# Three groups per half instead of four in the small transforms of a spectral filter, with buffers shared and the order of all engines searched anew

## The chip, the cores and the metric

One core of a Trainium2 chip runs the kernel. The metric is the device time of one execution in microseconds (us), the median of several. A core has five engines that run at the same time, each through its own list of instructions: PE (matrix multiply; its weight loads are listed apart as PEld), ACT and DVE (element by element, both can read PE's result memory PSUM), POOL, and SP, which here only issues DMA transfers. An engine takes its instructions strictly in the order of its list; where one needs the result of another engine or of a transfer, it waits for a semaphore, and everything behind it on the same engine waits too. PSUM has eight banks of 512 columns.

## What is computed

```python
x = A_x                                   # 1 x 2048 x 640, bf16
xn = (x - mean) / sqrt(var + 1e-5)        # over the 640
A = irfft2(rfft2(xn) * (w_r + 1j * w_i))  # over 2048 x 640, w_* are 2048 x 321
B = gelu(xn @ w1 + b1) @ w2 + b2          # w1 640 x 1536, w2 1536 x 640
out = x + A + B
```

## The kernel before

The 2048 rows are 16 chunks of 128 rows. `XN` is a chunk normalized, `xnT` its transpose (640 x 128, in five blocks).

Branch B: layer 1 (lines 735 to 754) goes through seven blocks of 1, 1, 2, 2, 2, 4 and 4 chunks; for each block and each of 12 units of 128 hidden columns it does five matmuls into one PSUM bank (`hps`, banks 4 to 7), and ACT writes gelu to `gT`. Layer 2 (`second`, line 905) makes a chunk's 640 outputs from the 12 hidden units, each a matmul of 512 and one of 128 columns, in four quarters of three units. A chunk in `KEEP` is summed ahead of time: its result is taken out of PSUM by DVE and added to the x that waits in float32 (line 921). For the others the last matmul of branch A is added in PSUM.

Branch A is the two-dimensional transform in steps. A-matmuls (line 724) transform the chunks along the rows, part one; `XV` holds their results. Then six B groups (line 773, `etab`) transform along the 640 columns; their results go to `Xb`. Then the small transforms: for each P of four, two C groups (line 794, `mtab`) turn `Xb` into a spectrum `Y`, DVE multiplies it by the filter (lines 819 and 823: two products into `T`, their difference and sum into `Z`), and two D groups (line 828, `ntab`) turn `Z` into `U`. A C or D group uses the 128 x 128 array as 16 tiles of 32 x 32: it is 32 matmuls in two sets of 16, of 322 columns (C) or 320 (D), one set added onto the other in four PSUM banks. ACT and DVE copy the four banks out, two instructions for C (644 columns each), four for D (512 and 128 columns). SP then transposes each half of a `U` by DMA into `XV` (line 844). When all 16 are in, six E groups (line 861, `getab`) transform back along the columns, DVE unfolds the result (lines 869, 874), and the H matmuls (line 928, `htab`) do the last step along the rows, chunk by chunk, into the PSUM banks where layer 2 may already lie; DVE adds x (line 930), and SP writes the chunk out.

Banks: B, C, D and E groups each take all four lower banks (0 to 3), so that each of them can start only when the copies of the one before it are done. Layer 1 has the upper four, layer 2 two of them at a time.

Order: nothing is scheduled while the kernel runs. Each `K.op` call makes one numbered operation; `ORDER` (line 159) lists the numbers for each engine, found by a search outside, and `Sched` (line 216) only gives out buffers and works out the semaphores. `CHAIN` (line 455) is the order of the groups on the lower banks:

```python
CHAIN = "b1 b0 c01 c00 b2 c10 d01 c11 d00 b4 b3 d10 d11 c20 c21 b5 c30 d20 d21 c31 d30 d31".split()
```

(as executed, c21 comes before c20). Between the groups PE does quarters of layer 2 and pieces of layer 1. At the start PE runs `WARM` = 38 and 12 matmuls on zeros (line 571), then a transpose of the bias b1 (line 647), then transposes chunks 0 and 1 itself (line 702, `tp`), while DVE makes the statistics of the chunks (line 661) as they land; chunks 6 to 15 are transposed by DMA (line 690, `TD`). The x for the final addition is written over `xnT` and `X` in float32 (line 897) and added to by a DMA from POOL (line 915), whose place in the order `WAVE` binds to the transposes of `U`.

Of the kernel before, what the change touches and what calls it, by code (L numbers as in the profile page):

```python
# [87 lines left out]
HOLD = 0.3  # L88
# [10 lines left out]
def mm_us(n):  # L99
    return max(n / 2400.0 + 0.0027, 0.0265)  # L100
# [24 lines left out]
class Pool:  # L125
# [34 lines left out]
    "sp": """8 12 13 14 15 16 17 18 19 25 20 43 28 46 32 31 24 23 27 33 37 164 166 29 48 179 190 177 192 38 49 42  # L160
30 44 40 39 203 205 219 217 36 34 35 47 26 45 41 524 523 548 522 547 545 521 546 569 572 571 50 51 570 595 596 594
593 622 613 658 649 639 675 685 694 757 731 711 766 748 721 782 798 791 805""",
    "pe": """115 7 52 114 112 120 118 231 234 235 270 232 237 238 273 274 271 267 268 279 280 282 283 285 286 276 243 277 240 244 241 246
# [8 lines left out]
709 763 776 746 777 764 719 778 792 785 779 786 787 780 788 793 789 794 795 796 799 800 801 802 803""",  # L172
    "act": """11 9 10 116 121 53 236 233 275 272 239 269 281 284 287 278 245 242 248 251 260 293 263 296 135 254 130 299 131 132 326 323
# [3 lines left out]
758 568 578 577 588 592 749 482 476 473 464 467 470 783 774 479 599 625 660 661 696 697 733 734 768 769""",  # L177
    "dve": """0 55 54 58 56 59 60 111 117 113 119 122 123 127 63 62 65 66 64 67 124 125 126 133 136 140 139 138 143 141 142 144
# [5 lines left out]
657 663 665 664 638 698 648 699 693 701 700 674 684 735 736 737 738 770 756 730 710 765 720 771 772 773 747 781 790 797 804""",  # L184
    "pool": """3 1 2 57 5 61 68 21 75 6 4 22 82 89 96 103 110 605 723 631 641 677 667 703 713 740 750 615 651 687 784 775
759""",
# [266 lines left out]
PRIO = {"hps": 23.0, "gelu": 27.0, "pb": 67.5, "pc": 50.5, "filt": 84.0, "ipc": 36.0, "eps": 80.0, "fin": 28.5}  # L453
AHEAD = 3
CHAIN = "b1 b0 c01 c00 b2 c10 d01 c11 d00 b4 b3 d10 d11 c20 c21 b5 c30 d20 d21 c31 d30 d31".split()
XASPLIT = ["01 23 4", "01234", "01234", "01234", "01234", "01234", "0123 4", "01 23 4"]
KEEP = (0, 2, 3, 5, 6, 8, 9, 10, 11)
HOME = tuple(sorted((KEEP + tuple(c for c in range(16) if c not in KEEP))[-8:], key=lambda c: (c not in KEEP, c)))
FOLD = (1.3, 1.8, -3.2, 66.3, 45.3, 69.8, 50.8, 17.3)
GP = (-81.0, 42.0, 4.0, 72.0, -32.0, 6.0, -9.0)  # L460
G1 = 1
WAVE = (0, 3, 0, 0, 2, 0, 0, 4, 0, 2, 0, 2, 4, 2, 2, 3)
WARM = (38, 12)


def bass_parallel_sum__spectral_gfnet__dense_activation_gelu__prompt_kernel(
# [21 lines left out]
    with ExitStack() as es:  # L488
# [48 lines left out]
        p_xn, p_x1, p_xf, p_xb, p_y, p_t, p_z, p_u = Pool(2), Pool(1), Pool(2), Pool(2), Pool(2), Pool(2), Pool(2), Pool(3)  # L537
# [37 lines left out]
        idle(WARM[0], WARM[0] * 0.103)  # L575
# [79 lines left out]
        for c0, n in [(0, 1), (1, 1)] + [(c, 2) for c in range(2, 16, 2)]:  # L655
            pr = 100 - c0 / 2
            B_mv, B_r = Buf("mv"), Buf("r")
            for c in range(c0, c0 + n):
                B_st = Buf("st")
# [8 lines left out]
        for pair in range(8):  # L668
# [10 lines left out]
            for n in range(2):  # L679
# [16 lines left out]
                for j0, j1, engs in ((0, 3, ["dve"]), (3, 5, ["act"])) if c < 2 else ((0, 5, ["dve", "act"]),):  # L696
# [8 lines left out]
                    if j0 and not c:  # L705
                        idle(WARM[1], WARM[1] * mm_us(128), gate=[tp])
# [30 lines left out]
        for bi, (c0, nt) in enumerate(BLOCKS):  # L737
            for fc in range(NFC):
                hps = Buf(f"hps{bi}_{fc}", psum, 1, ZONE["hps"])
                bg = Buf(f"gT{bi}_{fc}")  # L740
# [25 lines left out]
        def five_segs(n):  # L766
            return [("128", 4 * n * mm_us(Q4)), ("32", n * 0.12 - 0.05)]

        pb_ops, filt_ops, d_ops, v_ops = [], [], [], []
        B_v = [Buf(f"v{q}") for q in range(16)]  # L770
        B_xb = {}
        xb_at = {}
        for gi, (c0, n) in enumerate(GROUPS):
            xb = Buf(f"xb{gi}", p_xb)
# [4 lines left out]
            for i in range(n):  # L779
                B_xb[c0 + i] = xb  # L780
                xb_at[c0 + i] = lambda xb=xb, i=i: (xb.slot * 3 + i) * 2 * KP
            for v in range(2):
                K.op([("dve", dve_us(320 * n) + 0.05), ("act", act_us(320 * n) + 0.08 * n)], PRIO["pb"] - c0 / 10,
                     copy(lambda v=v, xb=xb, n=n: view(xb3, xb.slot * 6 * KP + v * (KP + 1), [[2 * KP, n], [1, 2], [2, Q4]]),
                          lambda v=v, bps=bps, n=n: psb(bps.slot + 2 * v, [[Q4, n], [512, 2], [1, Q4]])), reads=[bps], writes=[xb])
        zone = {f"b{gi}": o for gi, o in enumerate(pb_ops)}
        for P in range(4):
            two = (2 * P, 2 * P + 1)
            Ys, TBs, Zs, Us = [[Buf(f"{n}{pair}", p) for pair in two] for n, p in (("Y", p_y), ("T", p_t), ("Z", p_z), ("U", p_u))]
            tiles = [(pp, qq, hi, lo) for pp in range(2) for qq in range(2) for hi in range(2) for lo in range(2)]  # L790
            in_xb = list({id(B_xb[c]): B_xb[c] for c in range(4 * P, 4 * P + 4)}.values())
            for r in range(2):
                cps = Buf(f"cps{P}_{r}", psum, 4, ZONE["cps"])
                zone[f"c{P}{r}"] = pe([("small", 0.285)], PRIO["pc"] - P / 2 + 0.02 * r, lambda P=P, r=r, cps=cps: [
                    (psb(cps.slot + 2 * pp + hi, [[1, KP]], 0, 64 * qq + 32 * (lo ^ pp), 32),
                     part(mtab, 64 * hi + 32 * lo, 32, (P == pp == qq == hi == lo == 0) * 128 + v * 64 + r * 32, [[1, 32]]),
                     part(xb3, 64 * hi + 32 * lo, 32, xb_at[4 * P + 2 * pp + qq]() + v * KP, [[1, KP]]), v == 0, v == 1)
                    for v in range(2) for pp, qq, hi, lo in tiles],
                    reads=in_xb + [B_xbpad, B_m], writes=[cps])
                for pp, Y in enumerate(Ys):  # L800
                    K.op([("act", act_us(644)), ("dve", dve_us(644))], PRIO["pc"] - two[pp] / 5,
                         copy(lambda Y=Y, r=r: view(Yb, Y.slot * 4 * KP + r * KP, [[2 * KP, 2], [1, KP]]),
                              lambda cps=cps, pp=pp: psb(cps.slot + 2 * pp, [[512, 2], [1, KP]])), reads=[cps], writes=[Y])
# [169 lines left out]
```

## Time and profile before

| what | value |
|---|---|
| median of 3 runs | 149.65 us (149.59 to 150.43) |
| the profiled execution | 149.76 us |
| its span, first to last instruction | 147.8 us, 2.0 us lie around it |
| granted PE clock by the profile | 1.00 of full speed throughout |
| busy: PE, DVE, ACT, POOL | 142.2, 108.5, 86.5, 22.6 us |
| C groups: matmuls, mean of one | 256 of 32 x 322 columns, 301 ns |
| D groups: matmuls, mean of one | 256 of 32 x 320 columns, 308 ns |
| first layer-1 matmul, last matmul | 7.61 us, 145.1 us |

A line of the timeline has the start of a run of like instructions, its length to the end of the last, the engine, the line of the kernel, the operation, what is written from what, the shape and the number of instructions; in brackets the time the engine was idle before it, and what ended it. Neighbouring matmuls overlap in their pipeline, so the time that one holds PE is read from the start of the next. A few per cent of the matmul records can be missing. `ps<-Xb,mtab` is a C group, `ps<-Z,ntab` a D group, `ps<-etab,XV` B, `ps<-getab,XV` E, `ps<-xnT,W` layer 1, `ps<-W,gT` layer 2, `ps<-gtab,T` A, `ps<-Wf,htab` H.

### The profile page before, as it was taken

How to read it: one execution, taken by the hardware profiler on the slowest of the kernel's cores; microseconds unless marked ns; L12 is line 12 of the kernel's file. 1: busy time of each engine (PE TensorE's matmuls, PEld its weight loads, DVE VectorE, ACT ScalarE, POOL GpSimd, SP SyncE). 2: the span in 40 equal slices, each digit the busy share in tenths (PEclk: the TensorE clock that was granted, in tenths of full speed). 3: DMA queues.
4: the chain of work that ended last, by engine and by line, in shares of the span. 5: the costliest groups of instructions: out<-in, count | busy, mean ns of one | idle time of the engine just before them, and what ended most of it. 6: DMA issues, size and time to landing. Idle time of an engine off the chain costs nothing.

```text
span 147.8 us, 4200 instructions
## 1 busy us (share of the span) xinstructions
PE 142.2 (96%) x1760; PEld 93.9 (64%) x1778; DVE 108.5 (73%) x230; ACT 86.5 (59%) x161; POOL 22.6 (15%) x37
## 2 busy tenths in 40 slices
PE   7999999999999999999999999999999999999993
PEld 7889999899455455456545645555446666656572
DVE  2698999999944279699837695796202599989692
ACT  3179999789779977758366767304558244403000
POOL 1302430302200025100600004000019500000000
DMA  4999999898997631904656675995447993023315
GB/s 118 342 382 380 256 318 110 214 127 177 267 180 180 183 80 36 231 22 87 130 137 50 136 91 121 131 243 65 89 89 152 256 226 124 11 82 133 138 47 177
DMA packets 30890, 23.35 MB, mean 158 GB/s; under 512 B 19224, under 2 KB 27544, under 8 KB 30744
## 3 DMA queue, kind: packets, MB, share of 16 engines
q1 hardware_dynamic: 28336, 17.48, 50.9%
q0 software_dynamic: 2368, 5.57, 16.6%
q8 instruction: 14, 0.23, 0.6%
q10 hardware_dynamic: 168, 0.04, 0.1%
q14 instruction: 4, 0.03, 0.1%
HBM read 13.58 MB, written 2.62 MB: 110 GB/s over the span
## 4 chain that ended last, share of the span: by engine, by line
PE 94%; ACT 2%; issue 2%; DVE 0%
PE ps L546 93%; ACT gT L752 1%; PE ps L702 1%; ACT Y L557 0%; ACT xnT L557 0%; DVE W L930 0%; DVE warm L562 0%
## 5 line engine op out<-in xcount | busy, mean ns | idle before, releaser
L546 PE MATMUL ps<-xnT,W 128*128 128x256 bf16 (+2 forms) x420 | 57.8, 288 | 0.1
L546 PE MATMUL ps<-W,gT 128*128 128x128 bf16 (+3 forms) x380 | 55.2, 292 | 1.7 <-issue 1.0
L546 PEld LDWEIGHTS ps<-W,gT 128*128 128x128 bf16 x396 | 30.0, 98 | 23.9 <-issue 2.7
L546 PEld LDWEIGHTS ps<-xnT,W 128*128 128x128 bf16 x420 | 34.5, 98 | 14.9 <-issue 0.9
L752 ACT ACTIVATE gT<-ps,b1col 128x256 bf16<-128x256 f32 (+2 forms) x84 | 38.3, 508 | 9.5 <-PE ps L546 9.0
L557 ACT ACTIVATE Wf<-ps 128x960 bf16<-128x960 f32 (+1 forms) x10 | 8.5, 888 | 13.5 <-PE ps L546 13.5
L661 DVE BATCH_NORM_STATS2 stats<-X 128x6 f32<-128x320 bf16 x32 | 13.8, 473 | 2.1 <-DMA X<-in_A_x_dram 2.1
L915 POOL DMA_DIRECT2D X<-in_A_x_dram x8 | 7.1, 1134 | 44.5 <-DMA XV<-gtab 15.9
L819 DVE TENSOR_TENSOR T<-Y,Wf 128x1288 bf16<-128x1288 bf16 x16 | 12.5, 822 | 0.5 <-ACT Y L557 0.4
L558 DVE CAST Xb<-ps 128x960 bf16<-128x960 f32 (+1 forms) x7 | 7.9, 1141 | 3.9 <-PE ps L546 3.9
L915 POOL DMA_DIRECT2D xnT<-in_A_x_dram x8 | 7.5, 1742 | 19.9 <-ACT gT L752 19.9
L557 ACT ACTIVATE Y<-ps 128x644 bf16<-128x644 f32 x11 | 7.6, 705 | 5.0 <-PE ps L546 5.0
L665 POOL TENSOR_TENSOR rstd<-mv,mhalf 128x2 f32<-128x2 f32 (+1 forms) x9 | 6.3, 704 | 25.4 <-DVE mv L663 25.4
L558 DVE CAST Wf<-ps 128x640 bf16<-128x640 f32 (+1 forms) x2 | 2.0, 991 | 10.8 <-PE ps L546 10.8
L557 ACT ACTIVATE XV<-ps 128x1280 bf16<-128x1280 f32 (+3 forms) x10 | 9.3, 946 | 0.8 <-PE ps L546 0.8
L718 DVE TENSOR_TENSOR T<-T 128x128 bf16<-128x128 bf16 (+1 forms) x32 | 8.4, 308 | 0.1
L930 DVE TENSOR_TENSOR W<-ps,xnT 128x640 bf16<-128x640 f32 (+2 forms) x10 | 6.8, 688 | 2.0 <-PE ps L546 2.0
L546 PE MATMUL ps<-getab,XV 32*128 32x160 bf16 (+1 forms) x128 | 7.5, 242 | 0.0
L557 ACT ACTIVATE U<-ps 128x512 bf16<-128x512 f32 (+1 forms) x8 | 3.1, 434 | 7.5 <-PE ps L546 7.5
L921 DVE TENSOR_TENSOR X<-ps,X 128x640 f32<-128x640 f32 x8 | 6.5, 817 | 1.2 <-PE ps L546 1.2
L558 DVE CAST Y<-ps 128x644 bf16<-128x644 f32 x5 | 4.1, 828 | 4.2 <-PE ps L546 4.2
L714 DVE TENSOR_TENSOR T<-T 128x640 bf16<-128x640 bf16 x16 | 7.2, 479 | 0.1
(50 smaller groups left out, 140.7 us busy)
## 6 DMA issues: line engine op xcount, KB each, us to landing
X<-in_A_x_dram POOLq DMA_DIRECT2D x8, 320.0 KB, 4.3
xnT<-in_A_x_dram POOLq DMA_DIRECT2D x8, 320.0 KB, 7.1
W<-in_B_w_dram SPq DMA_DIRECT2D x5, 480.0 KB, 4.7
out_dram<-W SPq DMA_DIRECT2D x15, 160.0 KB, 1.8
X<-in_A_x_dram SPq DMA_DIRECT2D x7, 320.0 KB, 11.1
Wf<-in_A_w_i_dram SPq DMA_DIRECT2D x6, 160.5 KB, 4.9
Wf<-in_A_w_r_dram SPq DMA_DIRECT2D x6, 160.5 KB, 3.5
W<-in_B_w_dram SPq DMA_DIRECT2D x1, 800.0 KB, 7.9
```

The source lines that it names most:

```text
L546: ins = e.matmul(o_, lhsT=lw, rhs=rh, start=st, stop=sp_, skip_group_check=True)
L557: return e.activation(dst(), src(), ACT.Copy, scale=scale)
L558: return e.tensor_copy(dst(), src())
L661: st_op[c] = K.op([("dve", 0.393)], pr, lambda e, _, c=c, h=h: e.bn_stats(stats[:, c, 6 * h:6 * h + 6], view(X, c * D + H2 * h, [[1, H2]]) ...
L665: K.op([("pool", 0.65)], 500, lambda e, _, a=a, b=b: e.tensor_tensor(out=rstd[:, a:b], in0=mv[:, a:b, 1], in1=mhalf[:, a:b], op=ALU.pow), ...
L714: K.op([("dve", dve_us(640, 2))], pr, lambda e, _, k=k, op=op, xnv=xnv, x1v=x1v: e.tensor_tensor(out=x1v(H2 * k, [[D, 2], [1, H2]]), in0=x ...
L718: ring_ops.append(K.op([("dve", dve_us(4 * w, 2))], pr, lambda e, _, op=op, x1v=x1v, xfv=xfv, o_=o_, o0=o0, o1=o1, w=w: e.tensor_tensor(ou ...
L752: K.op([("act", act_us(128 * nt, 1))], pr + PRIO["gelu"] + GP[bi], lambda e, _, c0=c0, nt=nt, fc=fc, hps=hps: e.activation(gT[:, fc, 128 * ...
L819: filt_ops.append(K.op([("dve", dve_us(4 * KP, 2))], pr, lambda e, _, k=k, Y=Y, TB=TB, pair=pair: e.tensor_tensor(out=view(TT, TB.slot * 8 ...
L915: xo_ops[c] = K.op([("pool", 0.9)], 51 - c / 20, lambda e, _, c=c, xov=xov: e.dma_start(xov(0, D), xv[:, c, :], accum_op=ALU.add), reads=[ ...
L921: kept_ops.append(K.op([("dve", dve_us(D))], 30, lambda e, _, kps=kps, xov=xov: e.tensor_tensor(out=xov(0, D), in0=psb(kps.slot, [[1, D]]) ...
L930: K.op([("dve", dve_us(w))], 95, lambda e, _, os_=os_, fps=fps, o0=o0, w=w, xov=xov, base=base: e.tensor_tensor(out=view(W1, OST + os_.slo ...
```

## The change

- Each half (two P, four pairs) has three C and three D groups instead of four of each: a first of 484 columns (all 322 of the first spectrum part of one P and 162 of its second part), a middle one of 320 (the remaining 160 columns of both P), a last one of 484. Every group is 64 matmuls in four sets of 16, and four PSUM banks as before. Names are c00, c01, c02 for the first half and c10, c11, c12 for the second; the middle one is done first in the first half.
- The copies out become 968 columns for the wide groups; 640 for the middle one of C, which writes two `Y` at once. In D a wide copy is two instructions (768 and 192 columns), a middle one four (256, 64, 256, 64).
- `Z` is written over `Y`; `Y` has four buffers, `Zb` is gone. `xnT` serves as a third `Xb` buffer (after layer 1 of chunks 0 to 3; two memsets on POOL, after the same, clear its padding) and as a fourth `U` buffer (after layer 1 of chunks 4 and 5).
- `KEEP` has ten chunks instead of nine: 0 leaves, 12 and 13 come in. The float32 x of chunks 12 and 13 lies in `xnT` where the C groups of the second half read last, that of chunk 0 where a `U` was.
- The second warm-up has 6 matmuls instead of 12. The copies of A's results are split for other pairs (`XASPLIT`).
- `ORDER`, `CHAIN`, `WAVE` and the priorities are from a new search. On the lower banks PE now does b2 b1 b0 c01 c00 c02 b5 b3 d02 d01 d00 b4 c10 c11 c12 d10 d11 d12, then E. The last four y-copies that DVE makes are those of e0 to e3 (two before). PE transposes chunks 0 and 1 ahead of the bias. SP issues b2bc ahead of x6, one mirror and one direct load of the filter ahead of x8, and x10, w2_0 and ntab ahead of x14. POOL adds x for chunks 0, 14, 12, 13, 7, 15 last.

```diff
-CHAIN = "b1 b0 c01 c00 b2 c10 d01 c11 d00 b4 b3 d10 d11 c20 c21 b5 c30 d20 d21 c31 d30 d31".split()
+CHAIN = "b2 b1 b0 c01 c00 c02 b5 b3 d02 d01 d00 b4 c10 c11 c12 d10 d11 d12".split()
-KEEP = (0, 2, 3, 5, 6, 8, 9, 10, 11)
+KEEP = (2, 3, 5, 6, 8, 9, 10, 11, 12, 13)
-WAVE = (0, 3, 0, 0, 2, 0, 0, 4, 0, 2, 0, 2, 4, 2, 2, 3)
-WARM = (38, 12)
+WAVE = (4, 0, 0, 0, 2, 0, 0, 4, 1, 0, 0, 1, 4, 1, 1, 4)
+WARM = (38, 6)
...
-        Yb = sb("Y", [128, 2 * 4 * KP])
+        Yb = sb("Y", [128, 4 * 4 * KP])
-        Zb = sb("Z", [128, 2 * 4 * KP])
...
+        def xbt(slot):
+            return (xnT, 0) if slot == 2 else (xb3, slot * 6 * KP)
+        K.op([("pool", 0.1)], 60, lambda e, _: e.memset(view(xnT, KP - 2, [[2 * KP, 3], [1, 3]]), 0.0), writes=[B_xbpad], after=l1_tiles(0, 4))
...
+        CUT = 162
+        for h in range(2):
+            Ps, pairs = (2 * h, 2 * h + 1), [4 * h + i for i in range(4)]
...
+            def c_unit(cps, P, r, k0, n, at, v, first, last):
+                return [(psb(cps.slot + 2 * pp + hi, [[1, n]], at, 64 * qq + 32 * (lo ^ pp), 32),
...
+                t, o_ = ((gtab, 0), (TT, 16 * KP), (U2, 0), (xnT, 4 * D))[U.slot]
...
+            for g in range(3):
+                cps = Buf(f"cps{h}_{g}", psum, 4, ZONE["cps"])
+                units = [(Ps[0], 1, CUT, KP - CUT, 0), (Ps[1], 1, CUT, KP - CUT, KP - CUT)] if g == 1 else [(Ps[g // 2], 0, 0, KP, 0), (Ps[g // 2], 1, 0, CUT, KP)]
...
+                    m for v in range(2) for k, (P, r, k0, n, at) in enumerate(units) for m in c_unit(cps, P, r, k0, n, at, v, k == 0, True)],
...
+                    K.op([("dve", dve_us(2 * KP, 2))], pr, lambda e, _, TB=TB, Y=Y, r=r, op=op: e.tensor_tensor(
+                        out=view(Yb, Y.slot * 4 * KP + r * KP, [[2 * KP, 2], [1, KP]]), in0=tv(TB, 0, r), in1=tv(TB, 1, r), op=op), reads=[TB], writes=[Y])
...
+                units = [(Ps[0], 1, 1, 1, 0), (Ps[1], 1, 1, 1, Q4)] if g == 1 else [(Ps[g // 2], 0, 0, 2, 0), (Ps[g // 2], 1, 0, 1, 2 * Q4)]
+                d_ops.append(pe([("small", 0.345 if g == 1 else 0.475)], pr + 0.02 * (2 - g), lambda dps=dps, units=units, d_unit=d_unit: [
+                    m for r in range(2) for k, (P, v, par, n, at) in enumerate(units) for m in d_unit(dps, P, v, par, n, at, r, k == 0)],
```

More of the change, by code (lines that the diff above doesn't have):

```diff
@@ L87 @@
 SWITCH = 0.095
-HOLD = 0.3
+HOLD = 0.1
 def lag(t, size):
@@ L786, in bass_parallel_sum__spectral_gfnet__dense_activation_gelu__prompt_kernel @@
         zone = {f"b{gi}": o for gi, o in enumerate(pb_ops)}
[L787 to L803, printed above, removed]
@@ new lines, in bass_parallel_sum__spectral_gfnet__dense_activation_gelu__prompt_kernel @@
+        tiles = [(pp, qq, hi, lo) for pp in range(2) for qq in range(2) for hi in range(2) for lo in range(2)]
+        CUT = 162
+        for h in range(2):
+            Ps, pairs = (2 * h, 2 * h + 1), [4 * h + i for i in range(4)]
+            Ys = [Buf(f"Y{pair}", p_y) for pair in pairs]
+            Us = [Buf(f"U{pair}", p_u, 1, [(pair % 4, pair % 4 + 1)]) for pair in pairs]
+            TBs = [Buf(f"T{pair}", p_t) for pair in pairs]
+            def c_unit(cps, P, r, k0, n, at, v, first, last):
+                return [(psb(cps.slot + 2 * pp + hi, [[1, n]], at, 64 * qq + 32 * (lo ^ pp), 32),
+                         part(mtab, 64 * hi + 32 * lo, 32, (P == pp == qq == hi == lo == 0) * 128 + v * 64 + r * 32, [[1, 32]]),
+                         part(xb_at[4 * P + 2 * pp + qq][0], 64 * hi + 32 * lo, 32, xb_at[4 * P + 2 * pp + qq][1] + v * KP + k0, [[1, n]]),
+                         first and v == 0, last and v == 1) for pp, qq, hi, lo in tiles]
@@ L821, in bass_parallel_sum__spectral_gfnet__dense_activation_gelu__prompt_kernel @@
                         reads=[Y, B_wpad] + (B_w if pair == 7 else [B_w[k]]), writes=[TB], after=ring_ops))
+            for pair, Y, TB in zip(pairs, Ys, TBs):
+                pr = PRIO["filt"] - pair / 5
                 for r, op in enumerate((ALU.subtract, ALU.add)):
-                    K.op([("dve", dve_us(2 * KP, 2))], pr, lambda e, _, TB=TB, Z=Z, r=r, op=op: e.tensor_tensor(
-                        out=view(Zb, Z.slot * 4 * KP + r * KP, [[2 * KP, 2], [1, KP]]), in0=tv(TB, 0, r), in1=tv(TB, 1, r), op=op), reads=[TB], writes=[Z])
@@ L825, in bass_parallel_sum__spectral_gfnet__dense_activation_gelu__prompt_kernel @@
-            B_us = [Buf(f"u{pair}") for pair in two]
-            for v in range(2):
-                dps = Buf(f"dps{P}_{v}", psum, 4, ZONE["dps"])
-                d_ops.append(pe([("small", 0.285)], PRIO["ipc"] - P / 2 + 0.02 * (1 - v), lambda P=P, v=v, Zs=Zs, dps=dps: [
-                    (psb(dps.slot + 2 * pp + qq, [[1, H2]], 0, 64 * hi + 32 * lo, 32),
-                     part(ntab, 64 * qq + 32 * (lo ^ pp), 32, (P == pp == qq == hi == lo == 0) * 96 + 32 * ((0, 2), (1, 0))[v][r], [[1, 32]]),
-                     part(Zb, 64 * qq + 32 * (lo ^ pp), 32, Zs[pp].slot * 4 * KP + (2 * hi + r) * KP + v, [[1, 2], [2, Q4]]), r == 0, r == 1)
-                    for r in range(2) for pp, qq, hi, lo in tiles], reads=Zs + [B_n], writes=[dps]))
-                zone[f"d{P}{v}"] = d_ops[-1]
-                for pp, U in enumerate(Us):
-                    def evac(e, name, U=U, v=v, uv=uv, dps=dps, pp=pp):
-                        for o_, w in ((0, 128), (512, 32)):
-                            ins = copy(lambda: uv(U, o_ + 2 * w * v, [[D, 2], [w, 2], [1, w]]), lambda: psb(dps.slot + 2 * pp, [[512, 2], [Q4, 2], [1, w]], o_ // 4))(e, name)
-                        return ins
-                    K.op([("act", act_us(512) + act_us(128)), ("dve", dve_us(512) + dve_us(128))], PRIO["ipc"] - two[pp] / 5, evac,
-                         reads=[dps], writes=[U, B_us[pp]], after=a_ops + ring_ops)
@@ L841, in bass_parallel_sum__spectral_gfnet__dense_activation_gelu__prompt_kernel, with d_unit @@
-            for pair, U, B_u in zip(two, Us, B_us):
+                    K.op([("dve", dve_us(2 * KP, 2))], pr, lambda e, _, TB=TB, Y=Y, r=r, op=op: e.tensor_tensor(
+                        out=view(Yb, Y.slot * 4 * KP + r * KP, [[2 * KP, 2], [1, KP]]), in0=tv(TB, 0, r), in1=tv(TB, 1, r), op=op), reads=[TB], writes=[Y])
+            B_us = [Buf(f"u{pair}") for pair in pairs]
+            def d_unit(dps, P, v, par, n, at, r, first, Ys=Ys):
+                return [(psb(dps.slot + 2 * pp + qq, [[1, n * Q4]], at, 64 * hi + 32 * lo, 32),
+                         part(ntab, 64 * qq + 32 * (lo ^ pp), 32, (P == pp == qq == hi == lo == 0) * 96 + 32 * ((0, 2), (1, 0))[v][r], [[1, 32]]),
+                         part(Yb, 64 * qq + 32 * (lo ^ pp), 32, Ys[2 * (P % 2) + pp].slot * 4 * KP + (2 * hi + r) * KP + v + par, ([[1, 2]] if n == 2 else []) + [[2, Q4]]),
+                         first and r == 0, r == 1) for pp, qq, hi, lo in tiles]
@@ new lines, in bass_parallel_sum__spectral_gfnet__dense_activation_gelu__prompt_kernel, with evac @@
+            pr = PRIO["ipc"] - h
+            for g in range(3):
+                dps = Buf(f"dps{h}_{g}", psum, 4, ZONE["dps"])
+                units = [(Ps[0], 1, 1, 1, 0), (Ps[1], 1, 1, 1, Q4)] if g == 1 else [(Ps[g // 2], 0, 0, 2, 0), (Ps[g // 2], 1, 0, 1, 2 * Q4)]
+                d_ops.append(pe([("small", 0.345 if g == 1 else 0.475)], pr + 0.02 * (2 - g), lambda dps=dps, units=units, d_unit=d_unit: [
+                    m for r in range(2) for k, (P, v, par, n, at) in enumerate(units) for m in d_unit(dps, P, v, par, n, at, r, k == 0)],
+                    reads=(Ys if g == 1 else Ys[g:g + 2]) + [B_n], writes=[dps]))
+                zone[f"d{h}{g}"] = d_ops[-1]
+                for pp in range(2):
+                    parts = [(Us[pp], 3, 1, 0), (Us[2 + pp], 3, 1, Q4)] if g == 1 else [(Us[g + pp], 0, 3, 0)]
+                    wr = [b for U, *_ in parts for b in (U, B_us[Us.index(U)])]
+                    def evac(e, name, parts=parts, uv=uv, dps=dps, pp=pp):
+                        for U, b0, nb, at in parts:
+                            for o_, w in ((0, 128), (512, 32)):
+                                ins = copy(lambda: uv(U, o_ + w * b0, [[D, 2], [w, nb], [1, w]]), lambda: psb(dps.slot + 2 * pp, [[512, 2], [Q4, nb], [1, w]], at + o_ // 4))(e, name)
+                        return ins
+                    cols = [2 * nb * w for _, _, nb, _ in parts for w in (128, 32)]
+                    K.op([("act", sum(act_us(x) for x in cols)), ("dve", sum(dve_us(x) for x in cols))], pr, evac,
+                         reads=[dps], writes=wr, after=a_ops + ring_ops + (l1_tiles(4, 6) if any(Us.index(U) == 3 for U, *_ in parts) else []))
@@ L842, in bass_parallel_sum__spectral_gfnet__dense_activation_gelu__prompt_kernel @@
+            for pair, U, B_u in zip(pairs, Us, B_us):
                 for qq in range(2):
```

85 lines of the change are left out of this document (52 added, 33 removed), and 32 rows, old and new, of the table ORDER.

## The prediction

> **What bounds the kernel now.** I read the first part of the page for the engine that is full, then the chain that ended last, then PE alone in order of time, because a full engine can be full of waits. Last came the groups by shape, for prices.
>
> ```profile
> PE 142.2 (96%) x1760; PEld 93.9 (64%) x1778; DVE 108.5 (73%) x230; ACT 86.5 (59%) x161; POOL 22.6 (15%) x37
> PE 94%; ACT 2%; issue 2%; DVE 0%
> ```
>
> PE is 96% busy and carries 94% of the chain that ended last. What remains is to see whether PE streams or stalls.
>
> ```profile
> 50.63 0.38 PE L546 MATMUL ps<-xnT,W 128*128 128x512 bf16 x1
> 50.94 0.36 PE L546 MATMUL ps<-Xb,mtab 32*32 32x322 bf16 x16
> ...
> 50.94 0.50 PE L546 MATMUL ps<-Xb,mtab 32*32 32x322 bf16 x32
> 51.37 0.39 PE L546 MATMUL ps<-xnT,W 128*128 128x512 bf16 x1
> 73.63 0.52 PE L546 MATMUL ps<-Z,ntab 32*32 32x320 bf16 x32
> 74.31 0.43 PE L546 MATMUL ps<-W,gT 128*128 128x128 bf16 x2 [0.16 <-issue]
> ```
>
> These are PE's timeline in narrow windows, starts in the first column (the second line is from a window that ends at 51.05 and so holds only the first 16 matmuls of the group). A C group (`Xb,mtab`) holds PE from 50.94 to 51.37, 0.43 us; the 512-column matmul ahead of it held PE for 0.31 us, where such matmuls inside a dense run follow each other in 0.216 us (six in 1.30 us from 52.97 in the wider timeline): 0.09 us to enter. So a C group costs 0.52 us, of which 2 x 322 columns at 2.4 per ns are 0.27 and 0.25 is entry and exit. The D group (`Z,ntab`) at 73.63 seems to hold PE 0.68 us with 0.16 of waiting. But its successor begins with a 128-column half whose 512-column half isn't listed; 0.68 less 0.216 is 0.46, as other D groups read (60.34 to 60.79: 0.45). Those "issue" waits are missing records, not stalls. Adding every PE instruction by its price from the first layer-1 matmul at 7.61, I end 0.7 us before the real last matmul, 0.4 of which are two waits at 8.05 and 9.46. After 10 us PE practically never stalls: every nanosecond taken from PE's work counts, and every new wait too.
>
> ```profile
> 4.49 2.02 PE L546 MATMUL ps<-warm 128*128 128x128 bf16 x17
> 5.15 0.45 DVE L683 TENSOR_SCALAR T<-X,mv,rstd 128x640 bf16<-128x640 bf16 x1
> 5.75 0.45 DVE L683 TENSOR_SCALAR T<-X,mv,rstd 128x640 bf16<-128x640 bf16 x1 [0.15 <-POOL rstd L665]
> 6.56 0.67 PE L702 MATMUL ps<-ident,T 128*128 128x128 bf16 x7
> 7.61 0.90 PE L546 MATMUL ps<-xnT,W 128*128 128x128 bf16 x10
> ```
>
> The start, all engines in order of time. Warm-up matmuls follow each other at 0.107 us (half speed) up to 6.3 us, though the first normalized chunk was ready at 5.60; the transposes begin at 6.56 and layer 1 at 7.61, then at 0.056 us per matmul.
>
> **The change, part by part.** *C and D groups.* Removed: 16 groups of 2 sets of 16 matmuls; 8 x 0.52 (C) + 8 x 0.54 (D: 0.45 + 0.09) = 8.5 us. Added: 12 groups of 4 sets, widths 322/162/322/162 or 4 x 160: the same columns, four entries and exits fewer, 24 sets more. No row shows a 16-tile set of 160 columns. Lower bound of a set: its columns (162 are 0.0675 us) plus the 0.01 us by which one set follows another beyond its streaming (the first 16 matmuls end 0.36 us after 50.94, all 32 0.50 us after it: 0.145 us to a set, of which 322 columns are 0.134). Upper bound: 0.145 us whatever the width, if loading 16 weights and not streaming sets that pace. The nearest row is the tail of a B group (`etab,XV`), sets of four 32-row matmuls with 160 columns: a B group with three such sets holds PE 1.25 us (65.83 to 67.08 in the timeline), one with two 0.90 (81.46 to 82.36); of the 0.35 four full 160-column matmuls are 0.27, so a set is 0.08: with four tiles at least, 160-column sets do stream. I take 0.077 in C and 0.09 in D, whose operand has a stride of two. Then C: wide 0.09 + 0.145 + 0.077 + 0.145 + 0.21 (last set and exit) = 0.67, narrow 0.09 + 3 x 0.077 + 0.21 = 0.54; D, by the same with 0.155, 0.09 and 0.22: 0.71 and 0.58. Per half 2 x 0.67 + 0.54 + 2 x 0.71 + 0.58 = 3.88 against 4 x 0.52 + 4 x 0.54 = 4.24: -0.36, twice, less 0.1 for sets that I can't see: **-0.6 us**. At the upper bound a group costs 0.74 (C) or 0.78 (D, at 0.155) whatever its width: 12 x 0.76 = 9.1, **+0.6 us**; with the lower bound in D too, -0.8.
>
> [...]
>
> *Evacuations.* 16 Y copies of 644 columns become 8 of 968 and 4 of 640, U likewise; ACT (59% busy) and DVE (73%) do them. From the rows 960 wide and 644 wide a 968-wide Y copy is 0.98 on ACT, 1.17 on DVE. All B, C, D and E groups use the four lower PSUM banks, so each waits for the copies of the one before it, hidden only by the PE work that the new order puts between. Counting that work (0.216 per 512 columns, 0.815 per L2 quarter) against copies plus 0.15 to 0.2 us of signalling: b0 to c01 1.08 against 1.05; c01 to c00 1.51 against 1.0; c02 to b5 2.33 against 2.1 (both copies on ACT); b3 to d02 2.71 against 2.65 (both on ACT); b4 to c10 1.46 against 1.45; c10 to c11 1.46 against 1.32; d00 to b4 1.63 against 1.4; c12 to d10 3.96 against 3.8 of DVE filter work. The present order has pairs as tight (c01 to c00 1.08 against 1.0; b4 to b3 1.46 against 1.45) and shows no wait there. I put **+0.4 us** for what is late; bounds 0 and 3.
>
> *Z in place of Y, xnT as third Xb buffer and fourth U.* DVE computes the same 32 instructions; the in-place write follows both multiplies on the same engine: 0. The xnT regions are read last by layer 1 at about 40 us (chunk 0, unit 9) and first written at about 47: 0, the cover being 7 us of order. Two small memsets on POOL (0.12 each, as the Xb rows) lie ahead of its first accumulating DMA, which waits longer for ACT: 0.
>
> *One more kept chunk.* One more DVE addition (0.82), and chunks 12 and 13 have theirs in the last 35 us, with four `yo` copies on DVE instead of two: about 30 us of DVE work in the 33 us from E to the end, 26 in 32 now. Hidden by order; slack near 0.3 us at h3, h8 and h14. Inside the 0.4.
>
> *Start.* Six warm-ups fewer: the last ends at 5.7, not 6.3; tp0 then comes before the bias transpose. First copies need 5.70 + 5 x 0.107 + 0.25: about 6.5; layer 1 at 6.9 instead of 7.6. The first weights should be there (4.7 us by their row, after an issue at 1.66). Gain 0 to 0.7; next to be late are the third W1 load (layer 1 reaches it at 11.3; its row says 7.9 us after an issue at 3.40, 11.3) and gtab (8.7 after 3.88). On SP, b2bc (0.16 MB), one mirror and one direct filter load now stand ahead of x8, and w2_0 ahead of x14: x14 lands near 24.5 at some 260 GB/s, where DVE wants it at 24.1; slack at A7 is 0.65. I take **-0.5 us**.
>
> Sum against the profiled execution: span 147.8 and 2.0 around it, 149.76; -0.6 - 0.5 + 0.4 = -0.7: 149.06. The median of the runs is 0.1 lower, so **148.9 us**.
>
> **The rivals.** *Slower by a hand-over of the lower banks* (b3 to d02, b4 to c10, d10 to d11): the wider copies, several pairs of them on ACT alone, come late. The lower banks change hands 23 times; if the 11 hand-overs after a new group (all but the last one) are each 0.25 late beyond the forecast, PE loses 2.8 us: 151.7. It decides from about 0.2 us each. For it: margins of 0.0 to 0.3 above; against: the present order lives with the same.
>
> *Sets cost 0.145 us whatever their width*: -0.6 becomes +0.6, 150.1. For it: 16 weight loads of 0.088 us per set; against: the B tails.
>
> *The clock comes late.* Half speed ended during the transposes (seven of them from 6.56 average 0.075 us, between 0.107 and 0.056), some 5.8 us after the first warm-up matmul at 0.99; 5.3 us of that were warm-up, now 4.7. If full speed then came half as long again later, 2.9 us of work would run at half speed: +1.45, 150.3. Against: the transposes now follow at once, so PE is no less busy. [...]
>
> *More is won*: sets at their columns alone in both transforms (-0.8), the whole 0.7 at the start, no wait: -1.5 and more, 148.0. For it: the present order has no waits.
>
> **How the numbers follow.** A measurement of this kernel can tell about 1% from no change: 1.5 us, that is below 148.15 or above 151.15. Forecast 0.50 (148.2 to 149.9), more won 0.15, hand-overs 0.15, dear sets 0.12, late clock 0.08. Of these, more won is faster (with 0.01 from the forecast): 0.16; hand-overs slower (with 0.01 from dear sets): 0.16; the rest within 1%: 0.68. The range leaves out half of "more won" and most of the hand-overs: 148.1 to 150.9.
>
> **What would show it.** Right: 64 matmuls per C group, first group slot about 0.6 (wide) and 0.45 (narrow); first layer-1 matmul before 7.1; PE work ending about 1 us earlier. Wrong: a narrow group as long as a wide one; matmuls at 0.107 us after 7 us; real PE waits (no missing 512 half) for Y, U or Xb copies between 50 and 100 us, or for XV at 35, W's adders in the last 30.

## The result: 1.4% slower, and the profile after

The changed kernel takes 151.77 us, the median of five runs (151.12 to 152.30), beside 149.59 us for the kernel before on the same chip (five runs, 149.41 to 150.43): a ratio of 1.0137 (95% interval 1.0109 to 1.0166). The forecast was 148.9, with a range up to 150.9. The profiled execution took 151.25 us with a span of 149.1, which is 0.5 below the median of the runs; that of the kernel before took 149.76 with 147.8.

The first part of the page and the line of its queue q8, changed kernel:

```profile
PE 143.0 (96%) x2010; PEld 97.0 (65%) x2028; DVE 108.3 (73%) x226; ACT 87.4 (59%) x164; POOL 23.0 (15%) x39
...
q8 instruction: 16, 0.26, 0.7%
```

PE is as full as before, with 0.8 us more work. Next PE's waits after the first 20 us (engine waited for, total, times, longest), changed kernel:

```profile
PE ps L545 <- issue: 1.6, 10, 0.2
PE ps L545 <- DVE Wf L906: 0.2, 1, 0.2
```

The ten "issue" waits are missing records again, as the prediction read them; none of the waits is for `Y`, `U` or `Xb`. So the wider copies cost no hand-over, and the loss must lie in PE's own work. PE's timeline around a wide C group, a narrow D group and the start, changed kernel:

```profile
57.28 0.36 PE L545 MATMUL ps<-Xb,mtab 32*32 32x322 bf16 x16
...
57.28 0.42 PE L545 MATMUL ps<-Xb,mtab 32*32 32x322 bf16 x32
...
57.28 0.76 PE L545 MATMUL ps<-Xb,mtab 32*32 32x322 bf16 x48
...
57.28 0.83 PE L545 MATMUL ps<-Xb,mtab 32*32 32x322 bf16 x64
58.04 0.60 PE L545 MATMUL ps<-xnT,W 128*128 128x512 bf16 x2
...
73.17 0.77 PE L545 MATMUL ps<-Y,ntab 32*32 32x160 bf16 x64
74.10 0.43 PE L545 MATMUL ps<-W,gT 128*128 128x128 bf16 x2 [0.16 <-issue]
...
5.96 1.05 PE L701 MATMUL ps<-ident,T 128*128 128x128 bf16 x10
...
7.05 5.66 PE L545 MATMUL ps<-xnT,W 128*128 128x128 bf16 x91
```

The first four lines are the same group seen through windows that end after one, two, three and four sets of 16. The wide C group holds PE from 57.28 to 58.04: 0.76 us where 0.58 (0.67 with the entry) was forecast. The second set adds 0.06 to the end of the work, as columns would; the third adds 0.34. The D group of 4 x 160 columns holds PE 0.93, of which 0.216 belongs to a 512-column matmul whose record is missing: 0.71, hardly less than the wide C group's 0.76. The time from a group's first matmul to the start of the next 128-row matmul is called its slot below. Layer 1 begins at 7.05 instead of 7.61.

The start of each 17th, 33rd and 49th matmul and of the next 128-row matmul, in us from the group's first, by the records of the trace:

```
group                          17th   33rd   49th   next
C before, 2 sets of 322       0.148     -      -   0.428
C after, 322/162/322/162      0.147  0.332  0.467  0.762
C after, 4 x 160              0.079  0.264  0.398  0.692
D before, 2 sets of 320       0.155     -      -   0.442
D after, 320/160/320/160      0.156  0.341  0.485  0.791
D after, 4 x 160              0.086  0.271  0.403  0.710
```

The second set starts about when the first has streamed its columns, at 0.148 or 0.079: by the 0.216 us of 512 columns, 322 and 160 take 0.136 and 0.068. From there everything is nearly the same whatever the width: 0.185 us to the 33rd matmul, and then one every 8.35 ns (0.13 to 0.14 for 16), where within each of the first two sets they came at 3.35 ns.

What PE's time consists of, profiled execution against profiled execution (slots corrected by 0.216 where a record is missing, entries of 0.093 us each included):

| PE | before | after | difference |
|---|---|---|---|
| first layer-1 matmul | 7.61 | 7.05 | -0.56 |
| waits from there to 20 us | 0.42 | 0.69 | +0.27 |
| C groups: 8, then 6 | 4.17 | 5.02 | +0.85 |
| D groups: 8, then 6 | 4.34 | 5.14 | +0.80 |
| all else | | | -0.13 |
| last matmul ends | 145.35 | 146.59 | +1.23 |

### The profile page after: what moved, and what is told of

It is laid out like the page before. It is cut to its first block, busy times and chain, and to the rows that moved or that the text cites. A ratio compares the mean times of both kernels' runs of the same rounds, so it can differ in the third digit from the quotient of the medians.

```text
span 149.1 us, 4706 instructions
## 1 busy us (share of the span) xinstructions
PE 143.0 (96%) x2010; PEld 97.0 (65%) x2028; DVE 108.3 (73%) x226; ACT 87.4 (59%) x164; POOL 23.0 (15%) x39
## 4 chain that ended last, share of the span: by engine, by line
PE 82%; DMA 8%; SPq 3%; DVE 3%; issue 2%; DVEq 0%
PE ps L545 82%; DMA X<-in_A_x_dram 8%; SPq L540 3%; DVE Wf L557 1%; DVE W L967 1%; DVE stats L660 1%; PE ps L701 0%; DVE Wf L906 0%; DVE T L682 0%; DVEq L429 0%
## 5 line engine op out<-in xcount | busy, mean ns | idle before, releaser
L545 PE MATMUL ps<-xnT,W 128*128 128x256 bf16 (+2 forms) x420 | 58.4, 288 | 0.1
L545 PE MATMUL ps<-W,gT 128*128 128x128 bf16 (+3 forms) x380 | 54.5, 292 | 1.9 <-issue 1.4
L556 ACT ACTIVATE Wf<-ps 128x960 bf16<-128x960 f32 (+1 forms) x8 | 6.7, 869 | 20.6 <-PE ps L545 20.6
L556 ACT ACTIVATE xnT<-ps 128x640 bf16<-128x640 bf16 (+7 forms) x12 | 7.4, 651 | 6.7 <-PE ps L701 4.2
L556 ACT ACTIVATE XV<-ps 128x512 bf16<-128x512 f32 (+3 forms) x11 | 8.4, 776 | 0.6 <-PE ps L545 0.6
L717 DVE TENSOR_TENSOR T<-T 128x512 bf16<-128x512 bf16 (+1 forms) x32 | 8.5, 314 | 0.2
L556 ACT ACTIVATE Y<-ps 128x968 bf16<-128x968 f32 (+1 forms) x8 | 7.1, 904 | 2.5 <-PE ps L545 2.2
L556 ACT ACTIVATE Xb<-ps 128x960 bf16<-128x960 f32 (+1 forms) x5 | 5.8, 1186 | 3.2 <-PE ps L545 3.2
L682 DVE TENSOR_SCALAR T<-X,mv,rstd 128x640 bf16<-128x640 bf16 x16 | 6.7, 429 | 0.8 <-POOL rstd L664 0.7
L545 PE MATMUL ps<-etab,XV 32*128 32x160 bf16 (+1 forms) x128 | 7.2, 232 | 0.0
```

Source lines behind the costliest of these rows:

```text
L545: ins = e.matmul(o_, lhsT=lw, rhs=rh, start=st, stop=sp_, skip_group_check=True)
L556: return e.activation(dst(), src(), ACT.Copy, scale=scale)
L682: o = K.op([("dve", 0.356)], pr, lambda e, _, c=c, n=n, xnv=xnv: e.tensor_scalar(out=xnv(n, 0, [[1, D]]), in0=view(X, c * D, [[1, D]]), sc ...
L717: ring_ops.append(K.op([("dve", dve_us(4 * w, 2))], pr, lambda e, _, op=op, x1v=x1v, xfv=xfv, o_=o_, o0=o0, o1=o1, w=w: e.tensor_tensor(ou ...
```

## The experiments

**Theory**: the price of a group is set by its number of pairs of weight load and matmul; what comes after the 32nd pair comes late and slowly. **Rivals**: columns set the price, as forecast, and something else was lost; or a tile's third load of weights has to wait.

### c_pairs64: more pairs in the kernel before, nothing else

```diff
-  (psb(cps.slot + 2 * pp + hi, [[1, KP]], 0, ...), ..., part(xb3, ... + v * KP, [[1, KP]]), v == 0, v == 1)
-  for v in range(2) for pp, qq, hi, lo in tiles],
+  (psb(cps.slot + 2 * pp + hi, [[1, n]], a, ...), ..., part(xb3, ... + v * KP + a, [[1, n]]), v == 0 and a == 0, v == 1)
+  for v in range(2) for a, n in ((0, 162), (162, 160)) for pp, qq, hi, lo in tiles],
```

> The kernel before, with each matmul of its eight C groups cut into 162 and 160 columns: 64 pairs of weight load and matmul in a group instead of 32, the same columns, banks, copies and order. Theory (a group's price is set by its number of pairs): with 64 pairs a C group's slot goes from 0.427 us to that of the changed kernel's narrow C group, 0.69 us, eight times +0.26, so +2.1 us and a time of 151.7 us. Rival (a set of sixteen costs what its columns stream, as the prediction took it): the slot stays at 0.43 to 0.46 us and the time within 0.3 us of before, 149.6 to 149.9 us.

152.54 us, ratio 1.0219 (1.0196 to 1.0243). Five of the eight C groups hold PE 0.69 us and one 0.70, with their 17th, 33rd and 49th matmuls at 0.081, 0.266 and 0.399: the changed kernel's narrow group to within 2 ns, in the order and with the buffers of the kernel before. The other two hold it 0.80 and 1.38, so the eight come to 6.35 us instead of 3.42. The longest, in PE's timeline:

```profile
81.02 0.61 PE L546 MATMUL ps<-Xb,mtab 32*32 32x162 bf16 x46
82.16 0.31 PE L546 MATMUL ps<-Xb,mtab 32*32 32x162 bf16 x18 [0.53 <-issue]
```

After 46 matmuls PE is idle for 0.53 us, and no releaser is named: a second kind of loss, taken up below. Columns as the price are refuted: the same columns in twice the pairs cost 3.1 us, of which 2.1 are eight slots of 0.69 in place of 0.43 and 0.8 the two longer ones.

### c_pairs48: the same for half of the tiles

```diff
+  for v in range(2) for a in (0, 162) for pp, qq, hi, lo in tiles if pp == 0 or a == 0
+  for n in ((162, 160)[a > 0] if pp == 0 else KP,)],
```

> The same with half of the tiles cut: 48 pairs in a C group. Theory: pairs 1 to 32 go as before, the 33rd matmul starts 0.185 us after the 17th, and each later pair takes 8.35 ns, so 16 x 0.00835 = 0.13 us less than with 64 pairs: a slot of about 0.58 us, +1.2 us in all, 150.8 us. If the price came with each set of sixteen instead, whatever its number in the group, three sets in place of two would give 0.427 + 0.145 = 0.57 us too, but without a gap at the 33rd pair. Rival (columns): 149.6 to 149.9 us.

150.73 us, ratio 1.0089 (1.0070 to 1.0107). All eight slots are 0.584 to 0.586, eight times 0.157 more than before: 1.26 us, beside a loss of 1.33 between the medians. The 33rd matmul comes at 0.266 and the 48th at 0.418. In this order the 25th to 32nd matmuls have their tile's third weights, and the 25th starts 0.073 after the 17th, as the columns allow (0.068 for 160); the 33rd has only the second weights of its tile, and it is the one ahead of which the gap stands. So the third load is not what waits.

### halves: the pairs in another order

```diff
-  m for v in range(2) for k, (P, r, k0, n, at) in enumerate(units) for m in c_unit(...)],
+  m for half in range(2) for v in range(2) for k, (P, r, k0, n, at) in enumerate(units) for m in c_unit(...)[8 * half:8 * half + 8]],
```

> The changed kernel with the 64 pairs of each C group in another order: all four sets on the eight tiles of one half, then all four on the other half. It tells what the gap ahead of the 33rd pair hangs on. If on a tile's third load of weights: a gap of 0.185 us stands between the 9th and the 17th matmul (the third set of the first eight tiles), and again between the 41st and the 49th. If on the count (64 instructions are at hand when the group starts, and the rest comes 0.185 us after the 17th matmul and then at 8.35 ns a pair): the 17th matmul of a wide group follows the 9th by the stream alone, 0.07 to 0.08 us, the 33rd comes 0.185 us after the 17th, and from there on no two matmuls are closer than 8 ns.

A single execution, 151.51 us. In the wide groups the 9th starts at 0.147, the 17th at 0.217: 0.070 later, as by the stream (162 columns are 0.068) and against the third load. The 33rd starts at 0.332, and the pairs of the new tiles then come at 8.35 ns. One detail of my expectation fell: the 33rd comes 0.115 after the 17th, not 0.185; here it is 0.185 after the 9th, the first that had to wait for its tile. In c_pairs48 and in the other regular groups the 17th is that one; in merged_h1 (below) a group of 48 in a mixed order fits neither. That the gap's place goes by the count, and not by a tile's third load, is shown; what sets its length is open. Every run has as many weight loads as matmuls, so which of the two counts is open too. That 64 instructions are at hand when a group starts was my estimate, twice the 32 pairs ahead of the gap; the runs show the count alone.

### d_merged: fewer pairs in the changed kernel

The two units of a narrow D group have the same weights, so that one matmul can take both:

```diff
-  m for r in range(2) for k, (P, v, par, n, at) in enumerate(units) for m in d_unit(dps, P, v, par, n, at, r, k == 0)],
+  m for r in range(2) for k, (P, v, par, n, at) in enumerate(units[:1] if g == 1 else units) for m in d_unit(..., both=g == 1)],
...
-  ... + v + par, ([[1, 2]] if n == 2 else []) + [[2, Q4]]),
+  ... + v + par, ([[(Ys[2 + pp].slot - Ys[pp].slot) * 4 * KP, 2]] if both else [[1, 2]] if n == 2 else []) + [[2, Q4]]),
```

> The changed kernel, with the two units of each narrow D group, which have the same weights, taken by one matmul of 2 x 160 columns instead of two of 160: 32 pairs in place of 64, twice in the kernel; the columns and all else stay. Theory (pairs): the slot of these two groups goes from 0.71 us to the 0.445 us that the D groups of the kernel before have, twice -0.26, and the time from 151.8 to about 151.2 us. Rival (columns, or late hand-overs between the groups): no change, 151.6 to 151.9 us.

155.01 us, ratio 1.0386 (1.0360 to 1.0411): 3 us slower than the changed kernel, against both. The slots did fall as the theory has it (0.71 to 0.448 and 0.442). PE's timeline shows where it was lost, inside a narrow C group that the edit doesn't touch:

```profile
83.29 0.33 PE L545 MATMUL ps<-Xb,mtab 32*32 32x160 bf16 x24
83.40 0.25 PE L545 MATMUL ps<-xnT,mtab 32*32 32x160 bf16 x8
83.56 0.42 PE L545 MATMUL ps<-Xb,mtab 32*32 32x160 bf16 x23
85.77 0.24 PE L545 MATMUL ps<-Xb,mtab 32*32 32x160 bf16 x1 [1.80 <-issue]
...
86.02 3.17 PE L545 MATMUL ps<-xnT,W 128*128 128x512 bf16 x7
```

PE stops for 2.0 us in the middle of the group, and afterwards six 512-column matmuls take 0.427 us each instead of 0.216, 1.3 us more (the page's clock row has 77 in these two slices). No engine and no load is named as what PE waits for. The page lists a queue q8 of the kind `instruction`: 14 packets of 16 KB in the kernel before, for 3586 recorded PE instructions, and 16 in the changed kernel, for 4085, so 256 and 255 to a packet. By this count I take them for PE's code. By the records, one of them starts at 83.34 and takes 1.08 us; PE goes on 1.36 us after its end.

### merged_all and merged_shift: is it the code?

merged_all is d_merged with x6 loaded ahead of b2. Its C part had no effect: the records show 64 matmuls in both narrow C groups. merged_shift adds 88 PE instructions in the first 6 us:

```diff
-  [(psb(b.slot, [[1, 128]]), warm[:], warm[:], True, True) for _ in range(n)]
+  [(psb(b.slot, [[1, 64]]), warm[:], warm[:, 0:64], True, True) for _ in range(2 * n)]
```

> The changed kernel with fewer pairs and the same columns: the narrow D groups with one matmul for both units (64 pairs to 32), the narrow C groups the same where both tiles lie in one tensor (64 to 56 and 48 pairs), and the load of x6 ahead of that of b2. Theory (pairs): narrow D 0.71 to 0.445 us twice, narrow C 0.69 to about 0.62 and 0.56 us, and the wait of 0.26 us at 18.4 us gone: 0.53 + 0.20 + 0.26 = 1.0 us less than the changed kernel, 150.8 us. If the two-microsecond gap inside a C group that the kernel with merged D groups alone has comes from where the program's code blocks end, fewer pairs ahead of it move it, and it is shorter or gone; if it comes from the merged matmuls, it stays, and the time is 154 us. Rival (columns): 151.5 us.

> The kernel with the two merged D groups and x6 ahead of b2 (merged_all), with each filler matmul ahead of the first transposes cut into two of 64 columns: 44 more pairs, 88 instructions, in the first 6 us, and nothing else. Theory (the code of the tensor engine's queue comes in blocks of 256 instructions, and the gap of 3 us inside the second narrow C group stands where a block is used up while the transfer of the next one waits behind loads): the block's end moves by 88 instructions to an earlier place in the work, the request goes out ahead of the loads at 81 us, the gap goes, and the time falls from 153.8 to 150.8 to 151.2 us. Rival (the gap belongs to the merged groups themselves, or to a transfer that is late whatever the block's end): it stays at 2 to 3 us, 153.5 to 154 us.

merged_all: 153.82 us, ratio 1.0308 (1.0266 to 1.0351). The gap is still there, longer. Its timeline, and the DMA queues from 81.2 to 84.2 and from 84.2 to 85.4 us:

```profile
83.31 0.42 PE L545 MATMUL ps<-Xb,mtab 32*32 32x160 bf16 x23
86.58 0.22 PE L545 MATMUL ps<-Xb,mtab 32*32 32x160 bf16 x1 [2.85 <-issue]
```

```profile
DMA  0009997001519699699929669896999999999902
...
q1 hardware_dynamic: 630, 0.65, 165.8%
```

```profile
q1 hardware_dynamic: 22, 0.01, 11.1%
q8 instruction: 1, 0.02, 4.9%
```

The first row is how busy the DMA engines are in 40 slices. Up to 84.2 they carry the load of `htab` and the transposes of `U`, all on q1, the only queue listed (its share counts packets by their start and can pass 100%), and no code; PE has run dry at 83.7. By the records the last packet of `htab` ends at 84.33, the code packet goes from 84.33 to 85.28, and PE resumes 1.3 us later.

merged_shift: 153.55 us, ratio 1.0269 (1.0242 to 1.0296). The gap has moved, as the theory says, but it isn't gone, so my time was wrong. The C group at 83.73 has its plain 0.69 us; now PE stops after the third group:

```profile
87.46 0.38 PE L545 MATMUL ps<-W,gT 128*128 128x512 bf16 x1
89.55 0.72 PE L545 MATMUL ps<-W,gT 128*128 128x128 bf16 x4 [1.71 <-issue]
```

The packet starts at 86.19 and takes 2.07 us; PE goes on 1.3 us after its end, as in the other two (and 1.38 us after one in c_pairs64). The records also count it: PE stops after 2497 recorded instructions in c_pairs64, d_merged and merged_all alike, and after 2753 in merged_shift, 256 more, which is one packet. The 88 added instructions moved the place of the 2497th to 88 instructions earlier in the work, and there PE now goes on without a stop; the stop stands one packet later. That the gap goes by the count of instructions and ends 1.3 to 1.4 us behind a code packet makes the code its likely cause; why the packet starts late was seen beside busy engines only, not tested by itself.

### x6_first and merged_h1

```diff
-    "sp": """8 12 13 14 15 16 17 18 27 19 48 35 20 ...
+    "sp": """8 12 13 14 15 16 17 18 19 27 48 35 20 ...
```

merged_h1 has this edit too, and merges the narrow groups of the second half alone (D as above, C where both tiles lie in one tensor).

> The changed kernel with only the load of x6 ahead of that of b2. Theory (the statistics of x6 stand ahead of the normalising of tile 4 on the vector engine, and wait for a load that is 0.6 us later than before): the wait of 0.26 us ahead of the transposes at 18.4 us goes, 151.5 us. Rival (the transfers of the first 20 us are bound by their bytes, so another load is late in its place): 151.7 to 151.9 us.

> The changed kernel with x6 ahead of b2, and fewer pairs in the second half's narrow groups alone: C 64 to 48 pairs, D 64 to 32; the first half stays as in the changed kernel, so up to the second narrow C group the instructions are counted as there. Theory (pairs, and code blocks for the gap): no gap in that group, its slot 0.69 to about 0.56 us, the narrow D group 0.71 to 0.445 us, 0.4 us less than with x6 first alone, 151.5 to 151.1 us. Rival (columns): 151.5 us. If merged matmuls bring the gap: 154 us.

The wait at issue, in the chain of the changed kernel:

```profile
6.07 11.38 DMA X<-in_A_x_dram
17.47 0.89 DVE stats L660 x2
18.36 0.36 DVE T L682
18.76 0.45 PE ps L701 x5
```

x6 lands at 17.45 (15.10 before, by the records); its statistics stand ahead of tile 4's normalising on DVE, and PE waits 0.26 us. x6_first: 151.50 us, ratio 1.0122 (1.0095 to 1.0150), not told apart from the changed kernel. That wait is gone in its profile, but one of 0.68 us stands at 11.29, for the third part of W1 (below).

merged_h1: 152.06 us, ratio 1.0162 (1.0142 to 1.0182). No gap in the C group, so merging alone doesn't bring it. Slots of 0.627 with 48 pairs (0.56 expected) and 0.445 with 32, together 0.33 less. PE's waits show where more went:

```profile
PE ps L545 <- DVE W L970: 0.7, 1, 0.7
PE ps L545 <- DMA W<-in_B_w_dram: 0.5, 1, 0.5
```

At 135 us DVE waited 1.07 us for an output buffer whose store was late, and an E group waited for DVE. Why that store was late is open.

### The start: before_warm6, before_start, w1_ahead, x6_behind

All four are the kernel before with `WARM = (38, 6)`, six warm-up matmuls (fillers) in the second batch instead of twelve; three also change the order of the first loads on SP:

```diff
-    "sp": """8 12 13 14 15 16 17 18 19 ...        # x0 x1 W1 W1 x2 W1 gtab x4 x6
+    "sp": """8 12 13 14 15 17 16 18 19 ...        # before_start: gtab ahead of the third W1
+    "sp": """8 12 13 14 16 15 17 18 19 ...        # w1_ahead: the third W1 ahead of x2
+    "sp": """8 12 13 14 15 16 17 18 27 19 ...     # x6_behind: b2 ahead of x6
```

> The kernel before, with 6 instead of 12 filler matmuls ahead of the first transposes, and nothing else of the change. Theory (the fillers set the start, and nothing after it is waiting on data): six fillers at 0.107 us less, the first layer-1 matmul at 7.0 to 7.1 instead of 7.6 us, and some 0.4 to 0.5 us off the end: 149.1 us. Rival (the x loads set the pace of the first 20 us, and what starts earlier waits later): the gain is taken back at a transpose that waits for x6 or W1, 149.5 to 149.7 us.

> The kernel before with 6 fillers instead of 12 and with the third part of W1 loaded ahead of x2. With 6 fillers alone the first layer-1 matmul came 0.55 us earlier, and 0.44 us went back at 11.3 us, where it waits. Theory (what waits there is the third part of W1): that wait goes, and 0.4 us stay won: 149.1 us. Rival (x2 is then late for the transposes at 13 us, as all bytes of the first 15 us are needed): no gain, 149.4 to 149.7 us, with a wait at 12 to 13.5 us.

before_start's edit was another than its expectation says, by mistake: it put gtab, 0.5 MB, ahead of the third part of W1.

> The kernel before with 6 fillers, and the third part of W1 loaded ahead of x2; the run before_start was meant to do this, but its edit put gtab ahead of that part instead, 0.5 MB, and made the wait at 11 us longer by 1.2 us. Theory (the transfers of the first 12 us are bound by their bytes, so a load that is 0.3 MB further ahead lands some 0.8 us earlier): the wait of 0.44 us at 11.3 us goes, the first layer-1 matmul stays at 7.05 us, and unless the transposes of tiles 2 and 3 at 12.8 us wait for x2, the time is 149.0 to 149.2 us. Rival (x2 is then late by about 2 us for those transposes): a wait of 0.5 to 1.5 us at 12.5 to 13.5 us, and 149.5 to 150.5 us.

> The kernel before with 6 fillers, and b2 loaded ahead of x6, as the changed kernel does it. Theory (the 320 KB of x6 share the engines with the third part of W1, and in the changed kernel this part is in time because x6 goes later): the wait at 11.3 us shrinks from 0.44 to under 0.15 us, as in the changed kernel, and one of about 0.26 us for x6 appears at 18 to 20 us or not at all, since tile 4 is transposed 0.7 us later here: 149.1 to 149.4 us. Rival (loads issued after the third part of W1 do not slow it, and its landing scatters by half a microsecond from run to run): the wait at 11 us stays between 0.3 and 0.7 us, 149.5 us.

Measured: 149.50 us (ratio 1.0001, 0.9988 to 1.0015), 151.08 (1.0104, 1.0073 to 1.0135), 151.96 (1.0170, 1.0125 to 1.0216) and 149.83 (1.0014, 0.9994 to 1.0033). PE's timelines of before_warm6, before_start and w1_ahead:

```profile
7.05 4.44 PE L546 MATMUL ps<-xnT,W 128*128 128x128 bf16 x70
11.77 1.56 PE L546 MATMUL ps<-xnT,W 128*128 128x128 bf16 x25 [0.27 <-ACT gT L752]
```

```profile
9.82 1.34 PE L546 MATMUL ps<-xnT,W 128*128 128x128 bf16 x21
12.60 1.55 PE L546 MATMUL ps<-xnT,W 128*128 128x128 bf16 x25 [1.44 <-DMA W<-in_B_w_dram]
```

```profile
11.84 1.12 PE L546 MATMUL ps<-xnT,W 128*128 128x128 bf16 x17
15.41 0.81 PE L702 MATMUL ps<-ident,T 128*128 128x128 bf16 x10 [2.45 <-DVE T L683]
```

In before_warm6 layer 1 starts at 7.05, and stops at 11.3 until the third part of W1 is there. The second line names ACT, but by the records that part lands at 11.63, just before PE goes on. It lands at 11.29 in the kernel before, which doesn't reach it until 11.96, and at 12.46 with gtab ahead. Put ahead of x2 it lands at 11.25, but x2 at 12.08 instead of 9.05, and PE waits 2.5 us for tile 2. x6_behind does not shrink the wait (0.68 us; layer 1 starts at 6.76 there and the part lands at 11.66). So the loads set the first 12 us: an earlier start of layer 1 is given back there. Nor do the fillers alone set the start. PE's timeline of c_pairs48, which has all twelve:

```profile
6.58 4.52 PE L546 MATMUL ps<-xnT,W 128*128 128x128 bf16 x70
11.40 0.77 PE L546 MATMUL ps<-xnT,W 128*128 128x128 bf16 x11 [0.30 <-ACT gT L752]
```

Here matmuls go over from 0.107 to 0.056 us at 3.7 us, in c_pairs64 at 5.3 (layer 1 at 6.96), in the profile of the kernel before only at 6.8. c_pairs48 and c_pairs64 wait for W1 at 11 us as well, 0.46 and 0.33 us. None of the four versions with six fillers is faster than the kernel before, and no version here beats it.

## Why the prediction was wrong, by its steps

- **What bounds the kernel** held: PE, streaming, with missing records in place of stalls. The rest of the reading rests on it.
- **C and D groups: this step failed, and in its sign.** Forecast -0.6, measured +1.65. I priced a set of 16 by its columns and took the third and fourth set to go on like the second; what the runs show is a price by the number of pairs. With the entry, wide and narrow C groups cost 0.86 and 0.79 us (forecast 0.67 and 0.54), D 0.88 and 0.80 (0.71 and 0.58). Even the upper bound, 0.145 or 0.155 a set, was passed, because the 33rd matmul comes 0.185 after the second set's start. I took the price of a 160-column set from the tails of the B groups. They were nearest in width; in the number of instructions the nearest rows were the C groups themselves, with 32 pairs, and no row had more. Nothing in the trace of before went beyond the count where it turns.
- **Evacuations**: forecast +0.4 with bounds 0 and 3, measured 0, the lower bound. All margins held, even 0.0 at c10.
- **Z in Y, xnT as a buffer, the kept chunk**: 0 as forecast; PE's waits after 20 us are the missing records and 0.2 us.
- **Start**: layer 1 at 7.05, forecast 6.9; -0.56 there. That the six fillers brought this isn't shown: with all twelve, two other profiles have layer 1 at 6.58 and 6.96, so the 7.61 from which I counted was a late start, by when full speed came. Of the named followers W1's third part was just in time in the profiled execution (landed 11.24, wanted at 11.27), and x6, which I hadn't named, was late by 0.26 us. Net -0.29 where -0.5 was forecast. Seven of the other profiles with six fillers wait 0.33 to 0.68 us for W1 at this place, so that an ordinary execution probably wins nothing; this would be the 0.5 us between the profile and the median, but that is only argued.
- **Sum**: 149.76 + 1.65 - 0.29 = 151.1, beside 151.25 profiled. The price of the pairs is shown by adding them to the kernel before; taking pairs out of the changed kernel shortened the slots, but no run so far is clearly faster for it.
- **Rivals**: dear sets were the right one in kind, at 150.1 and a chance of 0.12; its price was too low. Hand-overs named 151.7, nearly the right time, by a mechanism that the waits exclude. The clock was not late: matmuls are 0.056 apart from 7 us on.

## What to carry to other kernels

Before cutting a group of small matmuls into more pieces, count its pairs: here 32 pairs were cheap, 0.43 us, and each set of 16 beyond them took 0.13 to 0.19, at 160 columns as at 322, so that three groups of 64 pairs cost more than four of 32. A price must come from a row that is near in every size that the change moves, and a range that rests on one size can lie wholly on the wrong side. And an engine that starts earlier gains only up to the next load that it needs: read when that load lands before counting the gain.

## What the runs showed of the hardware

- On 16 tiles the pairs of a set start 3.35 ns apart among the first 32 of a group, the later ones 8.35 ns apart, after a gap that stands ahead of the 33rd in every order tried (0.185 us after the 17th in the regular ones, 0.115 in halves). What holds the 33rd back, no run here shows.
- Queue q8 brings one packet of 16 KB for some 256 recorded PE instructions (14 for 3586 before, 16 for 4085 after). It is the likely cause where PE stops without a releaser: gaps of 0.53 to 2.85 us in four kernels, after 2497 recorded instructions or 256 later, each ending 1.3 to 1.4 us behind the end of such a packet. The profiles of the kernel before and of the changed one show no such gap.
- After one such gap (2.0 us between matmuls, d_merged) the granted clock was 0.50 for 3.4 us; in the profiles of merged_all and merged_shift, after 3.1 and 2.1 us, it stayed at 1.00. Two of merged_all's six executions, at 155.2 and 155.4 us beside 153.5 to 153.9, have a mean clock of 0.989, as d_merged has: one program can do both. What makes the difference is open.
